# Windowed attention into a two-layer network: the opening's list of steps in a new order

## The chip, the core and the metric

The kernel runs on one core of a Trainium2 chip. The metric is the device time of one execution in microseconds (us): the median of three runs. Five engines work side by side, each through its own queue in the order in which the program wrote it: TensorE (PE in the profile, its weight loads PEld), VectorE (DVE), ScalarE (ACT), GpSimd (POOL) and SyncE (SP, which here only issues transfers). POOL also issues transfers, among its own arithmetic.

## What is computed

```python
# q, k, v: (8, 8, 576, 64) float32: batch, heads, rows, width
scores = scale * q @ k^T                          # per batch and head
rel    = row - column;  keep 0 <= rel < 64        # causal window of 64
attn   = softmax(scores)
x      = attn @ v, heads side by side             # (4608, 512)
h      = x @ w_in                                 # (512, 2048)
g      = h * cos(h)
out    = g @ w_out                                # (4608, 512)
```

## The kernel before, in words

**Tiles.** The 4608 rows of x are worked in nine tiles of 512 rows (`mt`). For each tile TensorE computes h in 16 pieces of 128 columns (line 461, for the first tile line 425 in halves of 256 rows), ScalarE takes the sine, VectorE multiplies (the gate, `gT`), and TensorE multiplies by w_out. Attention runs ahead of the tile that needs it, in units of 64 rows of one pair of heads. A *group* is four units (some of batch 1 three), with one piece of PSUM for its scores.

**Two parts of the program.** From the second tile on, a planner with due times places the attention steps among the products. Everything before that, the *opening*, is written out as a list of steps, `FIRST`, one token each. The token's place in the list is its place in the queue of every engine that it uses. The opening loads batches 0 and 1 and both weight matrices, runs attention for batch 0 and batch 1, the whole first tile, and part of the attention of the second. The change is to this list.

**The tokens**, with the lines of their work:

- `Lq`, `Lk`, `Lv`, `Lwi`, `Lwo`: loads. `Lq0.0` and `Lk0.0` go out by SP (158), the others by POOL: pairs of heads of q and k for batches 0 and 1 (152), v in chunks of 128 rows (175), w_in in quarters (191), w_out in quarters (194), q and k of batch 2 in chunks of 96 rows (169). They cast to bf16 on the way.
- `tq`, `tk` (batch 0) and `Tq`, `Tk` (batch 1): 18 transposes on TensorE for a pair of heads (203); `pq`, `pk`, `Pq`, `Pk`: the copy out of PSUM (124, 225, 227). The last letter names the engine: `a` ScalarE, `d` VectorE, `p` POOL, `s` a transfer issued by SP.
- Batch 0, pair p, half g: `s.p.g.bank` scores with the mask added by TensorE (307, 314); `m` row maximum (324, one TENSOR_REDUCE); `e` exponentials with their sums (341); `i` reciprocal (351); `n` the normalisation w = e * 1/sum (358); `w` four transposes of the weights on TensorE (374); `c` the copy out (124).
- `v.a.g` (411) weights times values for two pairs of heads, `x.a.g` its copy to `xT` (124). `h.g.f.bank` one sixteenth of the first product of the first tile (eight matmuls, 425), `S` its sine, `g` its gate. `o.q.m.bank` (444): one quarter q of the second product for 128 rows m, four matmuls with w_out's quarter q, `oc` the copy out (124).
- Groups 8 (batch 0) and 9 to 18 (batch 1): `Gs`, `Gm`, `Ge`, `Gi`, `Gn` as above, with the maximum and the mask in one custom instruction for each unit (329). Then the weights are turned in one of two ways. A group that `DIRECT` names is turned on TensorE (`Gw`, 374) and copied out (`Gp`, 124). Any other is turned by a DMA transpose that SP issues (`Gc`, 377). `V.p` and `X.p`: values (393) and copy for the second tile.
- `z` and `y`: copies that spread v of batch 0 and of batch 1 into the odd chunks of its tile (186 by a transfer, 124 by an engine).
- `tb`, `tb2`: the loads of ScalarE's sine and exponential tables.

**What sets the order.** An engine takes its steps in list order and waits at each for its inputs and for a free buffer. Transposes and values share three PSUM buffers, scores and h five banks (the digit at the end of `s`, `h`, `Gs` and `o`). The second tile's first products follow the last token, on line 461.

Of the kernel before, what the change touches and what calls it, by code (L numbers as in the profile page):

```python
# [10 lines left out]
def _safe_warn(msg, *a, **kw):  # L11
# [22 lines left out]
T = 2 * Q  # L34
LAGS = (0.2, 1, 3, 3.2, 3.8)
SKEW = 3
DIRECT = (0, 7, 8)
OUTS = 3
FILL = (6, 12)
TURNED = {4: 2, 5: 2, 6: 2, 7: 6}  # L40
# [3 lines left out]


FIRST = (
# [18 lines left out]
)  # L65


# [1 line left out]
def kernel(  # L69
# [200 lines left out]
    last = n_listed + 4, n_listed + 5  # L270
    direct = set(range(n_first)) | {n_first + i for i in DIRECT} | set(last)

# [476 lines left out]
```

## Time and profile before

| | |
|---|---|
| median of three runs | 303.38 us (303.17 to 303.96) |
| the profiled execution | 304.26 us |
| its span, first to last instruction | 302.5 us |
| busy over the span | PE 290.5, DVE 233.8, ACT 232.2, POOL 208.7 us |
| PE in the first 20 of these us | 4.97 and 7.67 us of 10 |
| granted clock of TensorE | 1.00 |

The profile is of one execution, so single durations are read against its 302.5 us. A row of the timeline gives the start in us from the span's start, the time from the start of the first to the end of the last of its instructions, the engine, the line, the operation and its operands, and in brackets the engine's idle time ahead of it with what ended it. Durations overlap at their ends, so what an instruction costs its engine in a full queue is the distance to the next start.

### The profile page before, as it was taken

Reading aid. Unit: us, or ns where it says so; the run is one execution under the profiler, and the core shown is the slowest. Engines: PE = TensorE matmul, PEld = TensorE weight load, DVE = VectorE, ACT = ScalarE, POOL = GpSimd, SP = SyncE. Lnnn points to the kernel's source line nnn. Section 1 sums busy time; section 2 is a strip of 40 time slices with the busy share of each in tenths; the row PEclk is TensorE's granted clock in tenths of the full one; section 3 lists DMA queues with packets and bytes.
Section 4 is the critical chain, followed back from the end, with each engine's and each line's share of the span. In section 5 each row is a group of like instructions: output and inputs, shape, how many; then the busy total and the mean of one; then the engine's idle time right before and its main releaser. Section 6 shows DMA issues by size and latency. Waiting matters only on the chain.

```text
span 302.5 us, 8484 instructions
## 1 busy us (share of the span) xinstructions
PE 290.5 (96%) x2920; PEld 162.4 (54%) x2920; DVE 233.8 (77%) x913; ACT 232.2 (77%) x781; POOL 208.7 (69%) x238
## 2 busy tenths in 40 slices
PE   3889999999999999999999999999999999999995
PEld 2668844554454544545454445444544454785484
DVE  3898877988887886788668875887688658985893
ACT  5898698877987699869986999689978997305610
POOL 7899558996799779987999699878995860000000
PEclk9999999999999999999999999999999999999999
DMA  7999999999999994999999998999599944003013
GB/s 150 180 205 168 196 192 133 102 136 155 237 125 111 219 158 88 98 143 185 198 105 155 164 183 118 136 196 178 110 110 128 198 84 156 0 3 141 1 35 106
DMA packets 158588, 41.47 MB, mean 137 GB/s; under 512 B 146960, under 2 KB 154192, under 8 KB 158544
## 3 DMA queue, kind: packets, MB, share of 16 engines
q0 software_dynamic: 100192, 18.06, 83.8%
q1 hardware_dynamic: 58352, 22.85, 41.5%
q8 instruction: 23, 0.38, 0.5%
q14 instruction: 21, 0.17, 0.2%
HBM read 36.70 MB, written 9.44 MB: 153 GB/s over the span
## 4 chain that ended last, share of the span: by engine, by line
PE 84%; DMA 11%; POOL 3%; DVE 1%; issue 1%; POOLq 0%
PE h_ps L461 37%; PE out_ps L709 28%; PE out_ps L555 8%; DMA w_out<-in_moe_w_out_dram 7%; DMA q<-in_q_dram 4%; PE out_ps L444 3%; PE s_ps L292 3%; PE o_ps L393 3%; POOL w L358 2%; PE tq_ps L206 1%; PE tw_ps L374 0%; DVE xT L124 0%; PE s_ps L314 0%; POOL w_in L191 0%; DVE negm L324 0%
## 5 line engine op out<-in xcount | busy, mean ns | idle before, releaser
L461 PE MATMUL h_ps<-xT,w_in 128*128 128x512 bf16 x512 | 115.1, 379 | 0.2
L695 DVE TENSOR_TENSOR gT<-h_ps,sin 128x512 bf16<-128x512 f32 x128 | 85.1, 688 | 25.8 <-ACT sin L692 25.2
L692 ACT ACTIVATE sin<-h_ps 128x512 f32<-128x512 f32 x128 | 73.8, 598 | 37.0 <-PE h_ps L461 36.7
L341 ACT ACTIVATE e<-s,negm 128x128 f32<-128x128 f32 (+1 forms) x256 | 97.1, 381 | 2.9 <-DVE negm L329 1.9
L709 PE MATMUL out_ps<-w_out,gT 128*128 128x512 bf16 x384 | 85.3, 379 | 0.0
L358 POOL TENSOR_TENSOR w<-e,rden 128x512 bf16<-128x512 f32 (+1 forms) x68 | 69.0, 1031 | 19.3 <-DVE rden L351 14.8
L461 PEld LDWEIGHTS <-w_in 128*128 128x128 bf16 x512 | 49.0, 98 | 54.5
L709 PEld LDWEIGHTS <-gT 128*128 128x128 bf16 x384 | 36.5, 98 | 43.1
L329 DVE CUSTOM_DVE_ANT_0 s<-s_ps,mask 128x128 f32<-128x128 f32 (+1 forms) x256 | 56.0, 277 | 2.5 <-PE s_ps L314 2.2
L341 ACT ACTIVATION_READ_ACCUMULATOR e<-s,negm 128x1 f32 x256 | 47.9, 187 | 0.0
L169 POOL DMA_DIRECT2D q<-in_q_dram x36 | 28.6, 796 | 9.7 <-DMA q<-in_q_dram 3.2
L175 POOL DMA_DIRECT2D v<-in_v_dram x40 | 34.2, 869 | 0.8 <-DMA q<-in_q_dram 0.6
L169 POOL DMA_DIRECT2D k<-in_k_dram x36 | 28.5, 794 | 2.4 <-DVE negm L329 0.9
L351 DVE RECIPROCAL rden<-den 128x4 f32<-128x4 f32 (+1 forms) x73 | 12.1, 166 | 18.3 <-ACT e L341 18.1
L124 POOL COPY v<-v 64x1536 bf16<-64x1536 bf16 (+3 forms) x16 | 22.9, 1431 | 0.4
L329 DVE DVE_READ_ACCUMULATOR2_ANT negm<- 128x1 f32 x256 | 21.3, 83 | 0.0
L124 DVE CAST xT<-o_ps 128x512 bf16<-128x512 f32 x24 | 15.5, 679 | 4.6 <-PE o_ps L393 4.4
L444 PE MATMUL out_ps<-w_out,gT 128*128 128x512 bf16 x64 | 15.0, 379 | 1.0 <-DMA w_out<-in_moe_w_out_dram 1.0
L425 PE MATMUL h_ps<-xT,w_in 128*128 128x256 bf16 x128 | 14.6, 273 | 0.0
L555 PEld LDWEIGHTS <-sums 128*128 128x128 bf16 x128 | 12.1, 98 | 2.0 <-DVE sums L504 0.4
L425 PEld LDWEIGHTS <-w_in 128*128 128x128 bf16 x128 | 12.3, 98 | 1.4
L124 ACT CAST xT<-o_ps 128x512 bf16<-128x512 f32 x12 | 7.1, 590 | 6.7 <-PE o_ps L393 6.4
(85 smaller groups left out, 307.8 us busy)
## 6 DMA issues: line engine op xcount, KB each, us to landing
out_dram<-out_sb SPq DMA_DIRECT2D x16, 512.0 KB, 7.5
v<-in_v_dram POOLq DMA_DIRECT2D x32, 128.0 KB, 5.9
q<-in_q_dram POOLq DMA_DIRECT2D x36, 96.0 KB, 8.5
k<-in_k_dram POOLq DMA_DIRECT2D x36, 96.0 KB, 8.5
w_in<-in_moe_w_in_dram POOLq DMA_DIRECT2D x4, 512.0 KB, 9.4
w_out<-in_moe_w_out_dram POOLq DMA_DIRECT2D x4, 512.0 KB, 11.7
q<-in_q_dram POOLq DMA_DIRECT2D x7, 144.0 KB, 6.5
k<-in_k_dram POOLq DMA_DIRECT2D x7, 144.0 KB, 6.5
```

What stands on the lines that cost most here:

```text
L124: {"a": nc.scalar.copy, "p": nc.gpsimd.tensor_copy}.get(engine, nc.vector.tensor_copy)(out, in_)
L169: nc.gpsimd.dma_start(out=st[name, b][:, c].rearrange("p (h d) -> p h d", h=H), in_=src.rearrange("h p d -> p h d"))
L175: nc.gpsimd.dma_start(out=vt.rearrange("p (h d) -> p h d", h=H), in_=v[b, :, c * 128:c * 128 + n, :].rearrange("h p d -> p h d"))
L329: nc.vector.tensor_tensor_reduce(out=s[:, u, c], in0=s_ps[:, u, c], in1=mask[:, 2 - j % 2 if j else 0, c], scale=-scale if b else -1.0, sc ...
L341: nc.scalar.activation(e[:, u, c], s[:, u, c], AF.Exp, bias=negm[:, u:u + 1], scale=1.0 if n < n_first else -1.0, accum_out=den[:, u:u + 1])
L358: (nc.gpsimd if engine == "p" else nc.vector).tensor_tensor(out=w[:, 0:u], in0=e[:, 0:u], op=ALU.mult, in1=rden[:, 0:u].unsqueeze(2).to_br ...
L425: nc.tensor.matmul(out=h_ps[:, half * e:half * e + half], lhsT=w_in_sb[:, ks, ff * 128:ff * 128 + 128], rhs=st["xT", 0][:, ks, half * g:ha ...
L461: nc.tensor.matmul(out=st["h", ff], lhsT=w_in_sb[:, ks, ff * 128:ff * 128 + 128], rhs=st["xT", mt][:, ks], start=start, stop=stop)
L555: nc.tensor.matmul(out=to[:, e] if type(to) is not list else to[e], lhsT=lhs[name][f // 2][:, f % 2, 128 * e:128 * e + 128], rhs=rhs[name] ...
L692: nc.scalar.activation(sin, h_ps, AF.Sin, bias=math.pi / 2.0)
L695: nc.vector.tensor_tensor(out=gt[:, e], in0=h_ps, in1=sin, op=ALU.mult)
L709: nc.tensor.matmul(out=o_ps[e], lhsT=gT[ff // 2][:, ff % 2, ms * 128:ms * 128 + 128], rhs=w_out_sb[:, ff], start=ff == 0, stop=ff == n_ff - 1)
```

## The change

`FIRST` is replaced by another list of nearly the same steps, and `DIRECT` names two groups more.

- Order of the loads on POOL: q and k heads of batch 0 in another order; `Lwi.0` to `Lwi.2` stand behind and among normalisations, and not ahead of all of them; three chunks of q of batch 2 and two of v of batch 1 ahead of w_out's last quarter; one chunk of k of batch 2 directly behind it.
- Engines: of batch 0's normalisations `n.0.0`, `n.2.0` and `n.3.1` go from POOL to VectorE, of batch 1's `Gn.10`, `Gn.11`, `Gn.12`, `Gn.14` and of batch 0's last group `Gn.8`. `x.0.0` and `x.1.0` go from ScalarE to VectorE, `x.1.1` the other way. `zA.0` goes to POOL, `zB` from SP's transfers to POOL, `zC` from there to VectorE, `yA` to VectorE, `y.1` to POOL. `oc.0` goes to ScalarE. Some copies of q, k and weights change places between VectorE and ScalarE.
- TensorE's order: the first scores are those of pair 0's second half, behind the transposes `tq.1` and `tq.2`; `h.1.0` stands ahead of `h.0.4`; the parts of the second product that use w_out's last quarter stand later.
- Groups 11 and 14 are turned on TensorE.

```diff
-DIRECT = (0, 7, 8)
+DIRECT = (0, 3, 6, 7, 8)
...
 FIRST = (
-    "io Lq0.0 Lk0.0 mk cq.d mc ck.a tq.0 Lq0.1 pq.0.d Lk0.1 tk.0 pk.0.a s.0.0.0 Lq0.2 tq.1 tk.1 m.0.0 pq.1.a s.0.1.1 "
-    "Lk0.2 tq.2 pk.1.d s.1.0.2 Lq0.3 Lk0.3 tk.2 s.1.1.3 e.0.0 tq.3 m.0.1 Lq1.0 Lk1.0 Lq1.1 pq.2.d pk.2.d Lk1.1 tk.3 "
-    "m.1.0 s.2.0.4 Lv0.0 Lv0.1 Tq.0 Lv0.2 pk.3.d m.2.0 e.0.1 pq.3.a i.0.0 e.1.0 Tk.0 s.3.0.0 Tq.1 e.2.0 Lv0.3 Lwi.0 "
-    "Pq.0.d i.1.0 Lwi.1 m.3.0 m.1.1 i.2.0 Pk.0.a e.3.0 Lwi.2 Tk.1 n.1.0.p s.2.1.1 Pq.1.d Gs.10.2 m.2.1 Gs.9.4 "
-    "n.0.0.p Pk.1.a n.2.0.p i.3.0 e.1.1 w.0.0 zA.0.d w.1.0 c.0.0.d Gs.12.0 w.2.0 n.3.0.p i.0.1 c.1.0.d zA.1.d "
-    "c.2.0.d e.2.1 zB.0.s zB.1.s n.0.1.p i.1.1 w.3.0 v.0.0 c.3.0.d x.0.0.a s.3.1.3 Gm.10 v.1.0 m.3.1 i.2.1 Gs.11.2 "
-    "Gm.9 Gm.12 n.1.1.p x.1.0.a e.3.1 w.0.1 w.1.1 c.1.1.a i.3.1 h.0.0.1 h.0.1.4 tb n.2.1.p c.0.1.d Lwi.3 w.2.1 "
-    "h.0.2.0 n.3.1.p v.0.1 S.0.0 Gm.11 w.3.1 S.0.1 h.0.3.3 Lwo.0 S.0.2 c.2.1.d c.3.1.d v.1.1 zC.s g.0.0 S.0.3 "
-    "h.0.4.2 x.0.1.a x.1.1.d h.0.5.1 g.0.1 h.1.0.4 g.0.2 g.0.3 S.0.4 h.0.6.0 h.1.1.3 S.0.5 S.1.0 Lq1.2 S.0.6 g.0.4 "
-    "S.1.1 g.1.0 h.1.2.2 Lk1.2 Lq1.3 h.0.7.4 g.0.5 h.1.3.1 Lv1.0 Lwo.1 g.1.1 S.1.2 h.1.4.3 g.0.6 Lk1.3 S.0.7 h.1.5.0 "
-    "g.1.2 h.1.6.2 Lwo.2 g.0.7 S.1.3 S.1.4 S.1.5 Lwo.3 h.1.7.4 Lv1.1 S.1.6 g.1.3 g.1.4 S.1.7 g.1.5 Lv1.2 g.1.6 tb2 "
-    "Tk.2 Lv1.3 Pk.2.d Ge.10 Tq.2 Pq.2.d Tq.3 Ge.9 Ge.12 o.0.0.1 Pq.3.d o.1.0 Tk.3 Gs.14.3 Gs.13.0 Pk.3.d Lv0.4 "
-    "Lq2.0 Ge.11 Gi.10 Gm.14 g.1.7 Lq2.1 Lq2.2 o.0.1.2 Gi.9 o.2.0 Ge.14 Gn.10.p Gm.13 Gc.10 Gi.12 o.1.1 Gs.8.3 "
-    "Gs.16.4 Gm.8 o.3.0 Ge.13 o.2.1 Gi.11 oc.0.d Gn.9.p o.3.1 Gs.15.0 Gs.17.1 Gn.12.p o.0.2.3 Gi.14 Gm.15 oc.1.d "
-    "Gc.9 Gn.11.p Gi.13 Gm.16 o.1.2 Ge.8 Ge.16 Ge.15 y.1.d Gn.14.p yA.p Gi.8 Gc.12 Gm.17 o.0.3.0 Gi.16 Gn.13.p yB.p "
-    "Gc.11 Gn.8.p Lq2.3 Lq2.4 Lq2.5 o.2.2 o.3.2 o.1.3 Gn.16.d Gi.15 Gn.15.d Gw.8 Gc.14 Gc.13 Lk2.0 Gp.8.d Gw.16 "
-    "Lk2.1 Ge.17 Lk2.2 Gp.16.d Gi.17 Lk2.3 o.2.3 oc.2.a Gw.15 Gp.15.d V.0 V.1 V.2 V.3 Gs.18.4 X.0.a X.1.d X.2.a "
-    "X.3.d Gm.18 o.3.3 oc.3.d Ge.18 Gn.17.d Lk2.4 Gi.18 Gn.18.d Lk2.5 Lv1.4 "
+    "io mk mc Lq0.0 Lq0.1 cq.d Lk0.0 Lq0.2 Lk0.1 tq.0 ck.a tk.0 tq.1 pq.0.d pk.0.a tq.2 pq.2.a s.0.1.0 tk.1 "
+    "s.0.0.1 Lk0.3 Lq0.3 tk.3 Lk0.2 pk.1.a pq.1.d s.1.0.2 Lq1.1 Lk1.1 Lq1.0 Lv0.3 Lk1.0 m.0.1 m.0.0 Lv0.1 Lv0.0 "
+    "pk.3.d e.0.1 m.1.0 tq.3 e.0.0 Lv0.2 pq.3.d i.0.1 tk.2 pk.2.d e.1.0 n.0.1.p Lwi.0 s.3.0.0 Lwi.1 m.3.0 s.2.0.1 "
+    "e.3.0 m.2.0 Tk.1 s.2.1.4 s.1.1.2 Tq.1 i.1.0 i.0.0 Pk.1.d m.2.1 Pq.1.a Tq.0 e.2.0 s.3.1.3 Tk.0 Pk.0.a i.3.0 "
+    "n.0.0.d m.1.1 n.1.0.p n.3.0.p zA.0.p Lwi.2 Pq.0.d i.2.0 n.2.0.d zA.1.d m.3.1 Gs.10.1 w.2.0 Gs.11.0 w.1.0 "
+    "c.2.0.d e.1.1 w.0.0 i.1.1 c.0.0.d w.3.0 c.1.0.a Gm.10 e.2.1 c.3.0.d v.0.0 Gs.9.2 x.0.0.d v.1.0 zB.0.p "
+    "x.1.0.d Gs.12.1 n.1.1.p w.1.1 w.0.1 zB.1.p i.2.1 e.3.1 Gm.12 h.0.0.4 c.0.1.d i.3.1 n.3.1.d c.1.1.d h.0.1.1 "
+    "n.2.1.p w.2.1 Gm.11 Lk1.2 Lwi.3 w.3.1 v.0.1 tb Lq1.2 c.2.1.d Lk1.3 c.3.1.d h.0.3.3 S.0.0 x.0.1.a S.0.1 Gm.9 "
+    "v.1.1 x.1.1.a h.0.2.0 h.1.0.2 g.0.0 g.0.1 S.0.2 S.0.3 zC.d h.0.4.1 S.1.0 g.0.3 g.1.0 h.0.5.4 Tk.2 S.0.4 "
+    "S.0.5 h.1.1.3 Lwo.0 g.0.4 Lq2.5 Lq1.3 g.0.5 S.1.1 h.1.2.1 Pk.2.d g.1.1 h.0.6.2 Lwo.1 h.1.6.3 Tq.2 S.1.2 "
+    "h.1.3.4 S.0.6 g.1.2 g.0.6 g.0.2 Pq.2.d S.1.6 S.1.3 g.1.3 g.1.6 h.1.5.2 h.1.4.1 h.0.7.4 S.1.4 S.1.5 Lq2.4 "
+    "Lwo.2 Lv1.1 Lv1.3 Lq2.3 Lwo.3 Lk2.0 h.1.7.3 S.0.7 Tk.3 o.0.1.0 g.1.4 g.1.5 S.1.7 g.0.7 g.1.7 Gs.8.2 Gs.17.1 "
+    "o.1.1 Gs.13.4 Gs.14.3 Gm.17 Gm.8 Lv1.2 tb2 o.0.0.1 Tq.3 Pk.3.d o.1.0 o.0.2.2 Pq.3.d Ge.12 Gm.14 Gs.16.3 "
+    "Ge.10 Ge.8 Ge.14 Gi.10 Gi.12 Gn.10.d Gm.16 Gm.13 o.1.2 o.2.0 o.2.2 Gs.15.3 Gi.14 Lv1.0 Lq2.0 Lv0.4 Ge.9 yB.p "
+    "Lq2.2 Ge.16 Gn.14.d o.0.3.4 Gn.12.d Gi.8 Gi.9 Gm.15 Gn.8.d Gn.9.p Ge.13 Ge.11 Ge.15 Gw.14 o.2.1 Gi.16 o.1.3 "
+    "Gn.16.d Gi.13 yA.d o.3.0 Gn.13.p Gw.8 Gc.12 o.3.2 Gw.16 Gi.11 Gp.16.d o.2.3 oc.0.a Gn.11.d Gc.10 oc.2.a "
+    "Ge.17 Gc.9 Gc.13 Gi.15 Gp.8.d o.3.1 Gw.11 o.3.3 Gn.15.d oc.1.d Gw.15 Gs.18.0 y.1.p Gp.11.d V.0 Gp.15.d "
+    "Gp.14.a X.0.a V.3 X.3.a V.1 Gm.18 X.1.d Lq2.1 Gi.17 V.2 X.2.d Ge.18 Gn.17.d Gi.18 Gn.18.d Lk2.4 oc.3.d Lk2.5 "
+    "Lk2.1 Lk2.3 Lk2.2 Lv1.4 "
 )
```

## The prediction

> **What bounds the kernel now.** I read the page first, then the busy time by stretches, the chain that ended last, TensorE's waits, and the timelines of TensorE and VectorE over the opening.
>
> ```profile
> span 302.5 us, 8484 instructions
> ```
> ```profile
> 0.00:14.40 14.40, 7.99 (x223) 6.47 (x224) 8.45 (x18) 9.85 (x36) 11.62 (x24) 1.00 1.13 165
> 0.00:22.20 22.20, 14.60 (x385) 11.46 (x386) 15.51 (x46) 17.31 (x70) 18.67 (x32) 1.00 1.25 177
> 22.20:38.60 16.40, 16.40 (x226) 14.32 (x222) 13.74 (x41) 13.08 (x29) 12.00 (x16) 1.00 1.17 184
> 38.60:58.05 19.45, 18.49 (x217) 9.68 (x211) 15.22 (x78) 16.76 (x78) 15.28 (x18) 1.00 1.59 143
> 58.05:302.50 244.45, 241.02 (x2105) 126.96 (x2103) 189.37 (x755) 185.06 (x607) 162.78 (x174) 1.00 1.24 130
> ```
> Each row has the stretch, its length, then the busy time (with the count) of TensorE, its weight loads, VectorE, ScalarE and POOL, the granted clock, the DMA share and the GB/s. I cut at events: 22.20 is the first `h.0.0`, 58.05 the first product of the second tile. From 58.05 on TensorE works 241.02 of 244.45 us, and no token of the list stands there. So the list can move the end only by moving 58.05, and it moves it one to one. TensorE idles 7.60 us ahead of 22.20, nothing up to 38.60, and 0.96 us up to 58.05. What can be won lies in the first and the third stretch.
>
> ```profile
> PE tq_ps L203 <- DVE q L124: 4.0, 1, 4.0
> PE tk_ps L203 <- issue: 1.4, 1, 1.4
> PE out_ps L444 <- DMA w_out<-in_moe_w_out_dram: 1.0, 2, 0.6
> PE tw_ps L374 <- POOL w L358: 0.9, 2, 0.7
> ```
> ```profile
> 15.24 4.09 POOL w L358 x4
> ...
> 24.82 8.27 DMA w_out<-in_moe_w_out_dram
> ...
> 33.38 12.22 DMA w_out<-in_moe_w_out_dram
> ```
> The chain goes through POOL's normalisations, one each 1.02 us (4.09 / 4), which can't start before 15.24 because three loads of w_in stand ahead of them. Then it goes through w_out's quarters. The step from 33.09 (24.82 + 8.27) to 33.38 shows a rule of this program: POOL's last w_out load is issued when its first one has landed, and seven POOL loads stand between the two in the list. The nth load waits for the landing of the (n-8)th, and whatever POOL does behind it waits as well.
>
> **Part 1, up to `h.0.0`: VectorE's list.** The change takes the load off POOL: `n.0.1` ahead of w_in, two normalisations on VectorE. On POOL the chain to `v.1.0` is then short. But those two and both copies `x.0.0`, `x.1.0` are now VectorE's. Its list from the first maximum to `x.1.0` holds: 8 maxima, 5 copies of q or k, 6 reciprocals, 2 normalisations, 1 copy of v, 3 copies of weights, `Gm.10` (three units), 2 copies of x.
>
> ```profile
> 7.46 0.69 DVE L324 TENSOR_REDUCE negm<-s_ps 128x4 f32<-128x512 f32 x1 [1.97 <-PE s_ps L314]
> 9.46 0.69 DVE L324 TENSOR_REDUCE negm<-s_ps 128x4 f32<-128x512 f32 x1
> 12.44 0.75 DVE L124 COPY kT<-tk_ps 128x576 bf16<-128x576 bf16 x1
> 13.11 0.68 DVE L324 TENSOR_REDUCE negm<-s_ps 128x4 f32<-128x512 f32 x1
> 13.71 0.17 DVE L351 RECIPROCAL rden<-den 128x4 f32<-128x4 f32 x1
> 13.79 0.73 DVE L124 COPY qT<-tq_ps 128x576 bf16<-128x576 bf16 x1
> 17.77 0.65 DVE L124 COPY v<-v 64x512 bf16<-64x512 bf16 x1
> 19.18 0.29 DVE L124 COPY v<-v 64x512 bf16<-64x512 bf16 x1
> 54.12 0.69 DVE L358 TENSOR_TENSOR w<-e,rden 128x512 bf16<-128x512 f32 x1
> 54.73 0.68 DVE L124 COPY wT<-tw_ps 128x512 bf16<-128x512 bf16 x2
> ```
> ```profile
> L329 DVE CUSTOM_DVE_ANT_0 s<-s_ps,mask 128x128 f32<-128x128 f32 (+1 forms) x256 | 56.0, 277 | 2.5 <-PE s_ps L314 2.2
> L124 DVE CAST xT<-o_ps 128x512 bf16<-128x512 f32 x24 | 15.5, 679 | 4.6 <-PE o_ps L393 4.4
> ```
> From start to next start a copy of q or k costs 0.67 us (12.44 to 13.11), a maximum 0.60, a reciprocal 0.08, a normalisation 0.61. A copy of weights costs 0.34 (0.68 / 2), a unit on line 329 0.22 (56.0 / 256), a copy of x 0.65 (15.5 / 24). For the copy of v I take 0.29; 0.65 is its other end. The sum: 8 x 0.60 + 5 x 0.67 + 6 x 0.08 + 2 x 0.61 + 0.29 + 3 x 0.34 + 3 x 0.22 + 2 x 0.65 = 13.1 us.
>
> When does it start? Before, the first maximum ran at 7.46, behind `s.0.0`, which needs nothing that POOL loads. Now the first scores stand behind `tq.1` and `tq.2`, thus behind POOL's second load. In the trace the step that waits for POOL's second load is `tk.1`:
>
> ```profile
> 7.87 0.69 PE L203 MATMUL tk_ps<-ident,k 64*64 64x64 bf16 x18
> 8.37 0.62 PE L307 MATMUL s_ps<-mask,ident 64*64 64x512 bf16 x2
> 8.78 0.64 PE L314 MATMUL s_ps<-kT,qT 64*64 64x128 bf16 x8
> 9.21 0.69 PE L203 MATMUL tq_ps<-ident,q 64*64 64x64 bf16 x18
> ...
> 14.41 0.28 PE L203 MATMUL tk_ps<-ident,k 64*64 64x64 bf16 x7 [1.39 <-issue]
> ...
> 22.20 1.91 PE L425 MATMUL h_ps<-xT,w_in 128*128 128x256 bf16 x16
> ...
> 25.52 0.40 PE L374 MATMUL tw_ps<-ident,w 128*128 128x128 bf16 x4
> 25.75 1.04 PE L425 MATMUL h_ps<-xT,w_in 128*128 128x256 bf16 x8
> ```
> Transposes at 7.87, a group of scores 0.50 later, its maximum at 9.46: the same three steps in the same order stand in the new list, so the first maximum comes at 9.46, two us later than before. The second needs one more turn of transposes (0.50) and one more group (9.21 - 8.37 = 0.84), so it starts at 10.80, while VectorE is free at 10.06: 0.74 us idle. By the list's other waits VectorE is then always late: I find its inputs there ahead of it, POOL's two normalisations (`n.1.0`, `n.3.0`) and ScalarE's exponentials among them. So `x.1.0` ends at 9.46 + 13.1 + 0.74 = 23.3, and `h.0.0` starts near 23.4 instead of 22.20: **+1.2 us**.
>
> One stall moves with it. At 14.41 TensorE resumes after 1.39 us in which it waited for nothing visible, in the middle of 18 transposes, 223 matmuls from the start. If that goes by the count (the loading of its instructions would), it comes in `s.2.1` or `s.1.1`, holds `Tq.1`, which stands ahead of `e.2.0` on ScalarE, and so `n.2.0`. By that path I get 0.6 us more for VectorE; if it falls into an idle time, nothing. I take half: **+0.3**. `h.0.0` needs w_in's first quarter, whose issue moves behind `n.0.1`:
>
> ```profile
> 12.30 1.53 POOL L191 DMA_DIRECT2D w_in<-in_moe_w_in_dram x2
> ```
> ```profile
> DMA to landing us min/median/max: 8.3/8.3/8.3
> ```
> The second row is that of the first quarter: 12.30 + 8.3 = 20.6. Issued at about 14.5, behind the same fourteen loads, it lands between 20.6 and 14.5 + 8.3 = 22.8, below 23.4 at either end. SP's three copies of v go; they were ahead of nothing.
>
> **Part 2, 22.20 to 38.60.** TensorE is full here and stays so: the tokens are the same but for order, and `h.1.0` ahead of `h.0.4` gives w_in's third quarter 0.9 us more. Cost nothing; the cover is w_in's fourth quarter, issued some two us later than before, first used by `h.0.6` about four us later.
>
> **Part 3, 38.60 to 58.05.** w_out's waits, 0.96 us, go. A part `o` takes 0.87 us (57.18 to 58.05 below). The third quarter's first part was the fourth, now it is the seventh; the last quarter's was the sixth, now the twelfth: 2.6 and 5.2 us later, and 1.2 more by the lag. Against that stand, ahead of w_out's last quarter, 5 chunks more and one less: 3 of 96 KB and 1 of 128 KB net, 416 KB, at 184 GB/s 2.3 us, and some two us of later start. **-0.96**; at worst nothing is won. Groups 11 and 14 add 7 transposes, four in 0.23 us (25.52 to 25.75): **+0.40**. Their copies, five normalisations and one copy of v come to VectorE, `oc.0` and `y.1` leave it: about +2 us of its 19.45 - 15.22 = 4.2 us idle. Nothing on the path, cover thin. SP has four transposes instead of six.
>
> ```profile
> 57.18 1.04 PE L444 MATMUL out_ps<-w_out,gT 128*128 128x512 bf16 x4
> 58.05 2.75 PE L461 MATMUL h_ps<-xT,w_in 128*128 128x512 bf16 x12
> ```
> `V` now stands right ahead of line 461 with no part `o` between; `X.0` is copied beside `V.3`, `V.1`, `V.2`. Cost 0 to 0.2, taken as 0. **Sum**: 1.2 + 0.3 - 0.96 + 0.40 = +0.94 us. The span goes from 302.5 to 303.4. The profiled execution (304.26) lies 0.88 above the median of 303.38, so I add the difference to the median: **304.3 us**.
>
> **The rivals.**
>
> *Faster: VectorE's list is not the bound.* Should the second POOL load and the scores behind it be early enough for the first maximum at 7.46, the same 13.1 us end at 20.6, where w_in lands: -1.6 + -0.96 + 0.40 = -2.2, 301.2 us. It decides at a first maximum before about 8. For it: POOL's chain, the one seen in the profile, is really shortened. Against: the row at 7.87. Chance 0.10.
>
> *POOL and VectorE hold each other up.* The copies of v at 17.77 and 19.18 have one shape and cost 0.65 and 0.29 while POOL normalises throughout. And the one normalisation of VectorE that begins beside one of POOL takes longer for 384 columns (0.73) than the one at 54.12 for 512 (0.69):
>
> ```profile
> 52.52 1.03 POOL L358 TENSOR_TENSOR w<-e,rden 128x512 bf16<-128x512 f32 x1
> ```
> ```profile
> 53.24 0.73 DVE L358 TENSOR_TENSOR w<-e,rden 128x384 bf16<-128x384 f32 x1
> ```
> If two of VectorE's three new normalisations stand half a POOL one (0.51), and the copies 0.36: +1.4 on the path, 305.7 us. The Trainium skill, "SBUF — State Buffer", on the shared port pair, says that a VectorE instruction with two SBUF inputs and a GpSimd one that reads SBUF exclude each other, and the later one waits for the whole of the other; this speaks against putting normalisations on both. The two rows agree with it in part: 53.24 to 53.55 is the overlap, and about that much is the excess. Against the rival: POOL loads, too, in that stretch, so meetings are few. Chance 0.20.
>
> *The tail becomes late.* `Gn.13` stays on POOL behind loads that wait for landings, and its weights go by a DMA transpose:
>
> ```profile
> DMA to landing us min/median/max: 2.7/5.3/6.7
> ```
> I reckon `Gn.13` done at 52; with 5.3 us it is at 57.3, with 6.7 at 58.7, and `V.2` wants it near 58.6. With VectorE's thin cover: +1 us on top, 305.3. Chance 0.15.
>
> *It cancels.* No stall, 0.5 us less lag: 303.5, no change to be measured. Chance 0.10; the forecast has 0.45, its own range 303.7 to 305.0.
>
> **How the numbers follow.** A measurement tells 0.3% (0.91 us) from no change: 302.47 and 304.29. The forecast lies on the edge, so half of it is "same" (0.22) and half slower (0.23). Slower: 0.23 + 0.20 + 0.15 = 0.58. Same: 0.22 + 0.10 = 0.32. Faster: 0.10. The range leaves out the faster rival and the upper end of the two late ones: 302.6 to 306.2.
>
> **What would show it.** Right: the first TENSOR_REDUCE near 9.5; VectorE with hardly any idle from 11 to 23; first line 425 near 23.4 to 24; no wait of line 444 for w_out; 18 transposes where 11 were ahead of line 461; that line first near 59. Wrong: line 425 before 22.2, waits of line 444 or 393, or a gap ahead of line 461.

## The result, and the profile after

The changed kernel takes 312.14 us (median of 6 runs, 310.23 to 315.94), the kernel before beside it 303.27 (6 runs, 302.73 to 303.96): a ratio of 1.0285, 95% 1.0225 to 1.0345. The ratio leaves out the run of 315.94 as a slow one, over 1.5% above the fastest; the median of the other five is 311.24. The forecast was 304.3, in a range of 302.6 to 306.2. So the sign was right and the size was not: +8.87 us by the medians where I had written +0.94. The profiled execution took 313.04 us.

In the changed kernel every line number stands one higher (line 426 is `h`, 462 the later tiles' first product). Three views of its profile carry the reading: the span and clock on the page, the busy time by stretches cut at the same events, and TensorE's waits.

```profile
span 311.3 us, 8439 instructions
...
PEclk9978999999999999999979999999999999999999
```
```profile
0.00:27.03 27.03, 16.82 (x384) 13.46 (x386) 19.88 (x46) 18.59 (x77) 19.58 (x33) 0.87 1.12 156
27.03:43.92 16.89, 16.89 (x226) 14.34 (x223) 14.93 (x45) 10.96 (x20) 11.86 (x16) 1.00 1.11 156
43.92:62.89 18.97, 18.71 (x218) 9.83 (x217) 15.91 (x83) 17.48 (x80) 12.28 (x14) 1.00 1.63 137
62.89:311.30 248.41, 240.18 (x2082) 127.83 (x2104) 190.38 (x752) 185.49 (x608) 160.96 (x172) 0.99 1.22 127
```
```profile
PE s_ps L315 <- DVE qT L125: 3.9, 1, 3.9
PE o_ps L394 <- DMA wT<-w: 1.7, 1, 1.7
```
The stretches compare one to one with those of before: 27.03 against 22.20 (+4.83), 16.89 against 16.40 (+0.49), 18.97 against 19.45 (-0.48), 248.41 against 244.45 (+3.96); together +8.8, the difference of the spans. Two places lose in this execution: the opening, and one that I had called untouched. Each has one of the two long waits, and one of the two dips in the row PEclk.

**The opening.** The first fence is VectorE's timeline, the second POOL's, the third TensorE's, of the changed kernel; the fourth has the busy time of two stretches, in which the figure 1.00 or 0.50 is the granted clock.

```profile
8.85 0.69 DVE L325 TENSOR_REDUCE negm<-s_ps 128x4 f32<-128x512 f32 x1 [1.04 <-PE s_ps L315]
10.13 0.69 DVE L325 TENSOR_REDUCE negm<-s_ps 128x4 f32<-128x512 f32 x1 [0.59 <-PE s_ps L315]
...
16.07 3.37 DVE L359 TENSOR_TENSOR w<-e,rden 128x512 bf16<-128x512 f32 x1
19.36 0.68 DVE L325 TENSOR_REDUCE negm<-s_ps 128x4 f32<-128x512 f32 x1
19.96 0.74 DVE L125 COPY qT<-tq_ps 128x576 bf16<-128x576 bf16 x1
```
```profile
15.55 2.05 POOL L359 TENSOR_TENSOR w<-e,rden 128x512 bf16<-128x512 f32 x2
17.54 0.61 POOL L125 COPY v<-v 64x512 bf16<-64x512 bf16 x1
18.09 0.80 POOL L192 DMA_DIRECT2D w_in<-in_moe_w_in_dram  x1
```
```profile
20.76 0.53 PE L315 MATMUL s_ps<-kT,qT 64*64 64x128 bf16 x6 [3.92 <-DVE qT L125]
```
```profile
16.84:18.91 2.07, 0.00 (x0) 0.00 (x0) 2.07 (x1) 1.60 (x8) 2.07 (x4) 1.00 1.24 207
18.91:25.74 6.83, 4.70 (x66) 3.66 (x68) 6.07 (x18) 3.98 (x21) 3.49 (x3) 0.50 1.00 161
```
One normalisation, `n.0.0`, takes VectorE 3.37 us, 3.29 of them to the next start, where I had priced 0.61. It begins at 16.07, inside POOL's pair `n.1.0`, `n.3.0` (15.55 to 17.60), which the copy `zA.0` follows without a gap. Behind it VectorE has a maximum and the copy `Pq.0` of q, and on that copy TensorE waits 3.92 us. TensorE has nothing from 16.84 on; at 18.91 its clock is halved, and stays so for 6.83 us, five of them after work is there again.

**The middle.** The chain that ended last, around the values of the fifth tile, and the clock behind them:

```profile
149.48 1.04 POOL w L359
150.67 8.00 DMA wT<-w
158.67 0.04 issue
158.71 1.48 PE o_ps L394 x51
```
```profile
158.85:162.26 3.41, 3.19 (x56) 1.97 (x54) 1.95 (x4) 1.87 (x2) 1.83 (x2) 0.50 0.69 134
```
The code is the same here in both kernels. A DMA transpose of weights lands 8.00 us after its release; TensorE waits 1.7 us for it, and 3.41 us at half clock cost some 1.7 more (an estimate: half of them, since TensorE is full there): 3.4 of the 3.96 us. In the profile of before the same product begins without a wait, though the normalisation ahead of the transfer ends just as long before it: 145.61 to 151.46 there, 150.52 to 156.37 here, 5.85 us in both. So the transfer was slower, and not released later.

```profile
144.57 1.04 POOL L358 TENSOR_TENSOR w<-e,rden 128x512 bf16<-128x512 f32 x1 [0.48 <-DVE rden L351]
```
```profile
151.46 1.20 PE L393 MATMUL o_ps<-wT,v 128*64 128x64 bf16 x64
```
This loss is not a regular one. From the second tile's first product to the end the profile of before takes 244.45 us, and the profiles of the twelve other kernels below take 244.6 to 245.4, the variants of the changed list among them; only this one takes 248.41.

### The profile page after: what moved, and what is told of

Same layout as the page of the kernel before. It is cut to its first block, busy times and chain, and to the rows that moved or that the text cites. A ratio compares the mean times of both kernels' runs of the same rounds, so it can differ in the third digit from the quotient of the medians.

```text
span 311.3 us, 8439 instructions
## 1 busy us (share of the span) xinstructions
PE 292.6 (94%) x2895; PEld 165.5 (53%) x2927; DVE 241.1 (77%) x922; ACT 232.5 (75%) x782; POOL 204.7 (66%) x233
## 4 chain that ended last, share of the span: by engine, by line
PE 85%; DVE 4%; DMA 4%; ACT 3%; issue 1%; POOL 1%; POOLq 0%
PE h_ps L462 36%; PE out_ps L710 22%; PE out_ps L556 8%; PE h_ps L426 5%; PE out_ps L445 5%; DMA wT<-w 3%; PE o_ps L394 2%; PE s_ps L293 2%; ACT e L342 2%; DMA q<-in_q_dram 2%; PE tw_ps L375 1%; PE tq_ps L207 1%; PE s_ps L315 1%; DVE w L359 1%; DVE negm L325 1%
## 5 line engine op out<-in xcount | busy, mean ns | idle before, releaser
L710 PE MATMUL out_ps<-w_out,gT 128*128 128x512 bf16 x372 | 82.9, 379 | 1.7 <-issue 1.6
L359 POOL TENSOR_TENSOR w<-e,rden 128x512 bf16<-128x512 f32 x60 | 61.3, 1039 | 28.4 <-DVE rden L352 23.6
L125 POOL COPY v<-v 64x2048 bf16<-64x2048 bf16 (+3 forms) x19 | 26.4, 1389 | 0.6
L125 DVE CAST xT<-o_ps 128x512 bf16<-128x512 f32 x25 | 16.3, 679 | 6.6 <-PE o_ps L394 6.3
L445 PE MATMUL out_ps<-w_out,gT 128*128 128x512 bf16 x61 | 15.2, 380 | 0.3 <-issue 0.2
L125 ACT CAST xT<-o_ps 128x512 bf16<-128x512 f32 x11 | 6.3, 582 | 10.4 <-PE o_ps L394 9.1
```

What stands on the lines that cost most here:

```text
L125: {"a": nc.scalar.copy, "p": nc.gpsimd.tensor_copy}.get(engine, nc.vector.tensor_copy)(out, in_)
L359: (nc.gpsimd if engine == "p" else nc.vector).tensor_tensor(out=w[:, 0:u], in0=e[:, 0:u], op=ALU.mult, in1=rden[:, 0:u].unsqueeze(2).to_br ...
L710: nc.tensor.matmul(out=o_ps[e], lhsT=gT[ff // 2][:, ff % 2, ms * 128:ms * 128 + 128], rhs=w_out_sb[:, ff], start=ff == 0, stop=ff == n_ff - 1)
```

## The experiments

My theory after the traces: VectorE's normalisation is held up by POOL's arithmetic beside it, and the idle time that this gives TensorE halves its clock. The rival is the prediction's own reason, the late start and the length of VectorE's list. Where no other is named, the edit is to the changed kernel. For each, m0 is the start of the first maximum and h0 that of the first `h.0.0`; m0 to h0 is 14.74 us before (7.46 to 22.20) and 18.18 after (8.85 to 27.03). Behind the second maximum VectorE's longest wait is 0.56 us before and 0.59 after; from there to h0 it is 12.74 us before (9.46 to 22.20) and 16.90 after (10.13 to 27.03).

**a_pool: VectorE's three normalisations of batch 0 back on POOL.**
```diff
-n.0.0.d  n.2.0.d  n.3.1.d
+n.0.0.p  n.2.0.p  n.3.1.p
```


> The changed kernel with the three normalisations n.0.0, n.2.0, n.3.1 back on POOL. Theory 1 (a VectorE normalisation is held for as long as POOL works without a pause): no VectorE instruction of more than 1.2 us in the opening, first line 426 near 24 instead of 27.0, time 2.5 to 3.5 us below the changed kernel. Rival (the VectorE list is too long anyway, and the 3.37 us are an accident of that run): VectorE is 1.8 us shorter, line 426 at 25 to 26, 1 to 2 us gained.

VectorE's, POOL's and TensorE's timelines of this run:
```profile
18.38 2.15 DVE L125 COPY v<-v 64x512 bf16<-64x512 bf16 x1
```
```profile
16.10 3.05 POOL L359 TENSOR_TENSOR w<-e,rden 128x512 bf16<-128x512 f32 x3
19.08 0.62 POOL L125 COPY v<-v 64x512 bf16<-64x512 bf16 x1
```
```profile
21.57 0.40 PE L375 MATMUL tw_ps<-ident,w 128*128 128x128 bf16 x4 [2.50 <-POOL w L359]
```
310.48 us (310.37 to 310.93), ratio 1.0223 (1.0187 to 1.0258); m0 9.41, h0 26.75. The long normalisation is gone, but I had expected nothing over 1.2 us on VectorE and h0 near 24, and both missed: now its copy of v, 0.29 us at best, takes 2.15 beside POOL's train. And POOL's own weights come late. So the hold isn't special to normalisations, and giving the work back to POOL is no cure.

**b_clear: POOL's neighbours of `n.0.0` go to VectorE and ScalarE.**
```diff
-n.1.0.p n.3.0.p zA.0.p
+n.1.0.d n.3.0.d zA.0.a
```


> The changed kernel with n.0.0 still on VectorE, but POOL's neighbours gone: n.1.0 and n.3.0 on VectorE too, zA.0 on ScalarE. VectorE has 1.2 us more to do. Theory 1: n.0.0 takes 0.6 to 0.7 us instead of 3.37, line 426 starts near 24, 2.5 to 3.5 us gained. Rival (the list's length sets it): line 426 at 28, 1.2 us lost.

VectorE's and TensorE's timelines:
```profile
17.12 0.66 DVE L359 TENSOR_TENSOR w<-e,rden 128x512 bf16<-128x512 f32 x1
```
```profile
20.57 0.53 PE L315 MATMUL s_ps<-kT,qT 64*64 64x128 bf16 x6 [3.13 <-DVE qT L125]
```
The same `n.0.0` now takes 0.66 us: the hold, 3.37 - 0.66 = 2.71 us, is POOL's doing. The time is 309.30 (308.06 to 311.36), 1.0188 (1.0123 to 1.0252). h0 stays at 27.06, though: the first maximum came a microsecond later in this run (9.89), VectorE has two normalisations more, and TensorE still idles 3.13 us and its clock is halved again. Alone this run doesn't price the hold.

**c_swap: POOL's load ahead of its copy.**
```diff
-n.3.0.p zA.0.p Lwi.2
+n.3.0.p Lwi.2 zA.0.p
```


> The changed kernel with w_in's third load ahead of the copy zA.0 on POOL. It tells what holds VectorE: if only POOL's arithmetic does, n.0.0 comes free behind n.3.0, near 17.6, and ends near 18.2 instead of 19.36. If the issuing of a load holds it as well, n.0.0 ends at 18.9 or later and the time does not change by over 0.5 us.

VectorE's and POOL's timelines:
```profile
15.73 2.38 DVE L359 TENSOR_TENSOR w<-e,rden 128x512 bf16<-128x512 f32 x1
```
```profile
15.22 2.05 POOL L359 TENSOR_TENSOR w<-e,rden 128x512 bf16<-128x512 f32 x2
17.20 0.81 POOL L192 DMA_DIRECT2D w_in<-in_moe_w_in_dram  x1
18.01 1.60 POOL L125 COPY v<-v 64x512 bf16<-64x512 bf16 x2
```
Nothing but the order of two steps on POOL changed, and `n.0.0` is 0.99 us shorter: it ends at 18.11, so less its own 0.66 it began at 17.45, during the load's issue and ahead of the copy. So it was held by both normalisations and the copy, and the issue of a load lets it through. m0 to h0 falls to 16.90; 308.53 us (two runs, 307.85 and 309.21), 1.0156 (1.0096 to 1.0215). The swap and what went with it win back some 1.3 us of the opening's loss. In this profile the half clock lasts 3.41 us (21.1 to 24.5) and not 6.83, so some of the 1.28 can be the clock's.

**d_fill: the hold stays, TensorE is kept busy** by 12 matmuls whose result is overwritten.
```diff
+        for _ in range(12 if n == 10 else 0):
+            nc.tensor.matmul(out=s_ps, lhsT=ident, rhs=mask16[:, 0:4]..., start=True, stop=True, ...)
         if n == FILL[1]:
```


> The changed kernel with twelve extra matmuls of 512 columns (2.6 us at full clock) into the free bank ahead of Gs.10, so that TensorE does not idle for 3.9 us. Theory 2 (the idle drops TensorE to half its clock, and that costs on top of the held VectorE): granted clock 1.00 from 19 to 26, n.0.0 still 3.3 us, line 426 near 25.5, 1 to 1.7 us gained. Rival (VectorE sets the start whatever the clock): line 426 stays at 27, nothing gained.

Busy time by stretches and VectorE's timeline (lines stand three higher):
```profile
18.00:20.00 2.00, 2.00 (x11) 0.94 (x10) 2.00 (x2) 0.26 (x1) 2.00 (x3) 1.00 1.24 205
20.00:22.00 2.00, 1.15 (x13) 0.45 (x11) 1.94 (x5) 1.51 (x8) 0.49 (x1) 1.00 1.29 195
```
```profile
16.23 3.37 DVE L362 TENSOR_TENSOR w<-e,rden 128x512 bf16<-128x512 f32 x1
```
The hold is unchanged at 3.37, the clock is 1.00 throughout the opening, and m0 to h0 is 16.90 (9.00 to 25.90). So the half clock costs 1.28 us of the opening. 308.17 us (307.59 to 308.93), 1.0145 (1.0107 to 1.0184).

**clear_fill: the edits of b_clear and d_fill together.**
```diff
-n.1.0.p n.3.0.p zA.0.p
+n.1.0.d n.3.0.d zA.0.a
+        for _ in range(12 if n == 10 else 0): ...
```


> The run without POOL's neighbours (n.1.0, n.3.0 on VectorE, zA.0 on ScalarE) together with the twelve filling matmuls. If the held normalisation and the half clock are the two causes of the lost time ahead of h.0.0, the stretch from the first maximum to h.0.0 is 17.2 (without neighbours) less 1.3 (by the filling) = 15.9 us, against 18.2 in the changed kernel; time near 307. If a third cause is left, it stays above 16.8.

h0 comes at 25.08 (m0 9.00), thus 16.08 after the first maximum, where I had expected 15.9. 307.94 us (307.70 to 309.60), 1.0152 (1.0115 to 1.0190). The two edits take 18.18 - 16.08 = 2.1 us off, although VectorE has two normalisations more, 1.22 us at the prediction's price. And one hold is left, by POOL's copy `zB.0` of v. VectorE's and POOL's timelines:
```profile
17.26 2.12 DVE L362 TENSOR_TENSOR w<-e,rden 128x512 bf16<-128x512 f32 x2
```
```profile
17.35 1.48 POOL L125 COPY v<-v 64x1024 bf16<-64x1024 bf16 x1 [1.05 <-DMA v<-in_v_dram]
```
From the first start to VectorE's next instruction (19.30) the two normalisations take 2.04 us, 0.82 above their price. Without both, 16.08 - 1.22 - 0.82 = 14.04 us would be left, or 12.89 from the second maximum (10.15): an estimate of the changed list without hold and half clock. Before took 14.74 and 12.74, and the prediction had 13.94 (9.46 to 23.4). So the longer list is not what was lost.

**e_first: the first scores ahead of POOL's second load**, the rival's own test.
```diff
-tk.0 tq.1 pq.0.d pk.0.a tq.2 pq.2.a s.0.1.0 tk.1
+tk.0 pq.0.d pk.0.a s.0.1.0 tq.1 m.0.1 tq.2 pq.2.a tk.1
```


> The changed kernel with pair 0's first scores and their maximum ahead of the transposes that wait for POOL's first loads. By the forecast's step (the first maximum 1.4 to 2 us late, VectorE's list full behind it): first maximum near 7.5 instead of 8.85, line 426 about 1.2 us earlier, near 25.8. Rival (the held normalisation sets it, by POOL's unbroken work, which starts with w_in's loads): the first maximum is early, line 426 moves by under 0.5 us.

VectorE's and TensorE's timelines:
```profile
7.11 0.69 DVE L325 TENSOR_REDUCE negm<-s_ps 128x4 f32<-128x512 f32 x1 [1.52 <-PE s_ps L315]
...
9.85 0.69 DVE L325 TENSOR_REDUCE negm<-s_ps 128x4 f32<-128x512 f32 x1 [1.39 <-PE s_ps L315]
...
15.80 3.36 DVE L359 TENSOR_TENSOR w<-e,rden 128x512 bf16<-128x512 f32 x1
```
```profile
26.70 1.47 PE L426 MATMUL h_ps<-xT,w_in 128*128 128x256 bf16 x12
```
The first maximum comes 1.74 us earlier. But the second then waits 1.39 us for its scores and comes only 0.28 us earlier (9.85), `n.0.0` 0.27, and `h.0.0` 0.33. 309.76 us (309.00 to 310.59), 1.0198 (1.0169 to 1.0227). So an earlier first maximum alone is worth nothing, and the hold is there as before. The list behind it hardly moved, and what an earlier start of the whole list would be worth this run doesn't show.

**splice: before's list up to `h.0.0`, the change's steps behind it.**
```diff
 FIRST = (
-    (the changed list up to n.3.1.d, with h.0.0.4 in it)
+    (the list before up to i.3.1, then h.0.0 and all the changed steps that aren't in it yet)
```


> The list of the kernel before up to h.0.0, then the changed list's order and engines for all that is left, with groups 11 and 14 turned on TensorE. Theory 1 (the loss lies ahead of h.0.0): first line 425/426 near 22.2, w_out's waits gone, 11 more plus 7 transposes: second tile's first product at 57.6 to 58.1, time within 0.6 us of the kernel before. Rival (the second part is at fault too): 1 us or more above it.

TensorE's timeline:
```profile
22.00 1.91 PE L425 MATMUL h_ps<-xT,w_in 128*128 128x256 bf16 x16 [0.50 <-DVE negm L329]
...
25.80 0.44 PE L411 MATMUL o_ps<-wT,v 128*64 128x64 bf16 x16 [1.44 <-DMA v<-v]
```
305.97 us (304.74 to 306.24), 1.0059 (1.0033 to 1.0084); I had expected it within 0.6 us of before. Most of the loss is gone with the old opening. Most of the remainder, 1.87 us by the medians, is a wait that the splice itself makes: the old opening spreads v by a transfer, which the new order of values finds 1.44 us late.

**g_delay: before, with 24 such matmuls ahead of `h.0.0`**, to see what a late opening costs by itself.
```diff
+        for _ in range(24 if n == 11 else 0): ...
```


> The kernel before with 24 extra matmuls of 512 columns (5.2 us) on TensorE ahead of h.0.0, and nothing else. Theory 3 (what is lost ahead of h.0.0 goes to the end one to one, and a late start alone makes no further loss): 303.4 + 5.2 - up to 1.0 for w_out's waits = 307.6 to 308.6, line 461 near 62.3 to 63.3, granted clock 1.00 behind it. Rival (a shifted start makes the values of later tiles wait for their DMA transposes, as at 157 us in the changed kernel): some runs 2 us or more above that, with a clock under 0.99.

h0 moves from 22.20 to 26.95, by 4.75, and the time is 308.12 (307.61 to 309.04) against 304.10 beside it: +4.02, and 1.0147 (1.0114 to 1.0181). The waits for w_out, 0.96 us, go into the delay. So the opening counts one to one, less what it hides. Behind the second tile's first product this run takes 244.7 us, so a late opening by itself doesn't make the wait of the middle.

**h_tail: before, with the part of the second product that needs w_out's last quarter later.**
```diff
-... o.0.1.2 Gi.9 o.2.0 ... Gi.12 o.1.1 ... o.3.0 Ge.13 o.2.1 Gi.11
+... o.0.1.2 Gi.9 o.1.1 ... Gi.12 o.2.0 ... o.2.1 Ge.13 o.3.0 Gi.11
```


> The kernel before with two pairs of steps exchanged: o.1.1 ahead of o.2.0, o.2.1 ahead of o.3.0, so that w_out's third and fourth quarter are needed one part (0.87 us) later. The forecast's step on w_out: both waits gone, 0.9 us gained, 302.4 (0.997). Rival (the quarter lands later in other runs, or another wait takes its place): 0 to 0.4 us.

TensorE's waits and the chain that ended last:
```profile
PE o_ps L393 <- DMA wT<-w: 0.6, 2, 0.3
```
```profile
144.20 6.85 DMA wT<-w
```
Line 444 waits for w_out no more, and line 461 comes 34.76 us behind h0 (21.71 to 56.47), not 35.85. But 303.49 us (12 runs, 302.67 to 305.95) against 304.10 is 0.9993 (0.9971 to 1.0014): no difference. In the profiled run 0.6 us are given back at the middle's transposes.

**after_mid, best: the middle's group turned on TensorE**, in the changed kernel and in h_tail.
```diff
+    late = {n_listed + 2 * NU + 3}
+    direct = late | ...
+            if n in late:
+                at(T * b - 3.1, g_trans, n)
+                at(T * b - 3.05, g_put, n)
...
```


> The changed kernel with one group of batch 4 (the last of the four that the values for the fifth tile need) turned on TensorE, and no longer by a DMA transpose that lands within some 0.2 us of its use. Theory 3 (the spread of the changed kernel, 310.2 to 315.9, comes from those values waiting for that landing, and from the clock that halves behind the wait): 310.3 to 311.3 in nearly all runs. Rival (another cause): still runs of 313 to 316.

> The kernel before with o.1.1 ahead of o.2.0 and o.2.1 ahead of o.3.0, and with that one group of batch 4 turned on TensorE (0.23 us more). If the gain of the exchange (0.9 us at the start of the third tile) was given back at the values of the fifth tile, it now stays: 0.7 us below the kernel before (0.9977), with less scatter. If not, no difference.

TensorE's timeline of after_mid at the place of the middle's wait:
```profile
154.67 0.39 PE L376 MATMUL tw_ps<-ident,w 128*128 128x128 bf16 x4
...
156.71 1.37 PE L395 MATMUL o_ps<-wT,v 128*64 128x64 bf16 x64
```
The wait is gone from the trace: 309.89 us (308.52 to 310.99), 1.0198 (1.0163 to 1.0233), with no run over 311 where the changed kernel has four of six. But this doesn't show that the edit removed it: of the eight runs of a_pool and b_clear, with the transposes left as they were, only one was over 311, and no profile of theirs has the wait either. In best nothing is won: 303.41 (12 runs, 302.39 to 304.89), 0.9998 (0.9975 to 1.0020). No version here beats the kernel before by more than its interval.

**turn_two: before, with groups 11 and 14 turned on TensorE**, the change's other part by itself.
```diff
-DIRECT = (0, 7, 8)
+DIRECT = (0, 3, 6, 7, 8)
...
-... Gc.11 ... Gc.14 ... o.2.3 oc.2.a Gw.15
+... o.2.3 Gw.14 Gw.11 oc.2.a Gp.14.a Gp.11.d Gw.15
```


> The kernel before with groups 11 and 14 turned on TensorE, and nothing else. The forecast's step on DIRECT: 7 transposes, 0.40 us more on the path, nothing else late: 303.4 + 0.4. Rival (the copies and the three PSUM buffers make TensorE wait): 1 us or more. Other rival (two DMA transposes less free the others): no change.

304.17 us (10 runs, 303.19 to 307.37) against 303.65: 1.0035 (1.0002 to 1.0069). The medians differ by 0.52 us, near the 0.40 of the prediction, but the interval, 0.1 to 2.1 us, also holds the rival's 1 us.

## Why the prediction was wrong, step by step

The step that failed is in Part 1. It priced every instruction of VectorE as though POOL did nothing beside it, so `n.0.0` at 0.61 us, and it gave TensorE's clock no term. In the runs POOL held `n.0.0` for 2.71 us, and the half clock behind the wait cost 1.28. The step that took the time from 58.05 on as untouched failed too, by 3.4 us, but in the profiled execution only.

- **What the list can move.** Up to the second tile one to one: right, by g_delay. "From 58.05 on TensorE works 241.02 of 244.45 us, and no token of the list stands there" was true, but not that therefore nothing is lost there. 3.4 us of the profiled execution are a transfer's. Whether the changed list makes this wait more frequent isn't shown: a wait over 0.6 us stands there in one only of the thirteen profiles of kernels other than before. The granted clock is on record for each of the changed kernel's six runs, 0.976 to 0.994, and doesn't tell which of them had it: the run of 314.71 and that of 310.42 both have 0.987.
- **The start of VectorE's list**, the step I called the cause: the first maximum came at 8.85, not 9.46, and the second at 10.13, not 10.80. The order of the three steps was right; the second load landed earlier than the row at 7.87 had it. Against before, the second maximum is 0.67 us late, and e_first doesn't settle what that is worth.
- **Its length**, 13.1 us and 0.74 idle to `x.1.0`, `h.0.0` right behind: 13.94. Without hold and half clock some 14.0 are left, by the estimate at clear_fill. So the sum of the rows held, as far as that estimate goes.
- **POOL and VectorE hold each other up.** This rival had the mechanism, with a chance of 0.20, and the wrong price: half a normalisation of POOL, 0.51, twice, and 0.36 for the copies. The hold of `n.0.0` is 2.71, because it goes on over POOL's next instructions: the list has `n.1.0.p n.3.0.p zA.0.p` right behind `n.0.0.d`. The Trainium skill, "SBUF — State Buffer", section "Terms", on the shared port pair, has the loser block until the other's instruction is over. The trace agrees that it blocks, and shows more: in the changed kernel the waiting normalisation isn't served between two instructions of POOL back to back. The profile of before gave no warning of that. There POOL does six normalisations without a gap, and the copy of v at 17.77, which the prediction shows, took 0.65 us in their midst; it was served before the next of them was over. Why VectorE is let in there and not in the changed kernel stays open. POOL's timeline of before:

```profile
15.24 6.13 POOL L358 TENSOR_TENSOR w<-e,rden 128x512 bf16<-128x512 f32 x6
```

- **TensorE's clock.** No step of the prediction had it: 1.28 us of the opening (d_fill) and some 1.7 in the middle. In the opening of before TensorE also idles, 4.0 us, but at the very start. The Trainium skill, "TensorE: Matmul & The Clock Gate", section "What's actually happening", gives windows of 3413 ns, after an idle one of which the clock is halved. The lengths here agree, 6.83 being two of them and 3.41 one; an idle window was not needed, since the clock fell 2.07 us after the last matmul. The price isn't the same in every run: the run of 311.24 us has a mean granted clock of 0.994 over its 309.5 us, which is some 3.7 us at half clock in all (an estimate), less than the 6.83 of the profiled opening.
- **The stall with the count**, +0.3: it isn't among TensorE's waits any more. Whether it went or lies within the 3.92 us can't be told.
- **Part 2**, cost nothing: +0.49.
- **Part 3**, -0.96 + 0.40: the waits for w_out went, and the stretch is 0.48 shorter, forecast 0.56. The extra transposes fit what I had said, but the interval of turn_two is wide. And the waits of before were not worth 0.96 on the average: h_tail removes them and wins nothing that can be measured; turn_two's profile has 0.4 us of them.
- **The tail becomes late**: no wait ahead of line 462 is in the trace.

By size, in the profiled executions: 4.83 at `h.0.0`, of which 0.67 is the later second maximum, 2.71 the hold, 1.28 the half clock and 0.17 the rest (an estimate, since hold and clock were measured in different runs and need not add up); 0.01 up to the second tile; 3.96 in the rest, of which 3.4 is the transfer's and the clock's behind it.

## What to carry to other kernels

Before a step that works within SBUF goes to VectorE (here normalisations, and a_pool's copy of v), read what POOL does at that moment, and allow for a hold as long as POOL's whole unbroken run of arithmetic, not one instruction of it; a load's issue in between (c_swap) is a cheap way out. Where a forecast has a wait of TensorE in mid-work, give the half clock behind it a price and a chance: it followed waits of 1.7 us (the middle) and of 2.5 to 4.4 us (the openings), and in the profile of best even waits of 1.34 and 0.37 (3.41 us at half from 19.0 on), though not the one of 1.44 in splice's profile at 25.80. A stage whose busy share is full still has transfers that land just in time; list their margins before calling it untouched.

## What the runs showed of the hardware that I had not expected

- A normalisation on VectorE beside a train of POOL: 3.37 us, 2.38 with the train cut by a load's issue, 0.66 without neighbours. A copy of v from SBUF to SBUF on VectorE: 2.15 us beside such a train, 0.29 at best. Each ended 0.8 to 1.3 us after POOL's last arithmetic, somewhat more than its own length; spans of POOL are rough, so the difference isn't explained. In the midst of six normalisations of POOL in before, such a copy took 0.65.
- The hold goes both ways: POOL's copy of v of 64x1024 took 1.48 us beside VectorE's normalisations in clear_fill and 1.03 without them, at 24.28 in the changed kernel.
- TensorE's clock is given back late: 6.83 us at half, though matmuls were there again after 1.85 (18.91 to 20.76).
- DMA transposes of weights take very different times to land: 8.00 us in the middle of the changed kernel, 6.85 in h_tail, and 2.4 to 9.4 over the whole profile of before.
